# Fixed tiles for pairs and single banks, router constants inside a planned order, and new ranks in an attention, routing and gated-layer kernel

## The chip, the cores and the metric

One core of one Trainium2 chip runs the whole program. The metric is the device time of one execution in microseconds (us), lower is better; several runs are taken and their median is quoted.

## The reference

Inputs `q, k, v, a_re, a_im` have shape (4, 8, 768, 48): batch, heads, sequence, head width. A complex, decaying state per head is stepped along the sequence, then tokens are sent to experts, and a gated layer follows.

```python
mag = np.sqrt(a_re * a_re + a_im * a_im)
scale = np.minimum(mag, 0.999) / (mag + 1e-06)
a_re_n, a_im_n = (a_re * scale, a_im * scale)
for t in range(S):
    new_re = ar * S_re - ai * S_im
    new_im = ar * S_im + ai * S_re
    S_re, S_im = (new_re + k_t v_t^T, new_im)
    y[:, :, t] = q_t @ S_re
...
logits = x @ w_gate            # x: 3072 tokens x 384
# pairs (token, expert) in falling order of logit; each expert takes 384 tokens
out[mask] = np.maximum(x[mask] @ w1[e], 0.0) @ w2[e]
...
return ((x @ w_a) * (x @ w_b)) @ w_out
```

## The kernel before

**Stages.** `whole` calls `make_router` (constants and small tiles of the routing), then `attention`, then `moe_glu` (experts and gated layer, eight phases). The change touches the first two.

**How attention is tiled.** The sequence is cut into 6 chunks of 128, the batch into 2 pairs, so there are 12 steps `i` (NB), each with 2 units `n` (24 units). For each step `gates` (L304) loads a_re, a_im, q, k and v and forms logarithms and angles: `ln`, `rec`, `rho`, `g`, `e`, `th` on ScalarE and VectorE (L331, L334, L338). `sums` (L352) takes running sums along the chunk by matrix products: the sum of logarithms `LL` (L376 to L389, by the helper on L361) and of angles `HH` (L395 to L398); each holds a pair of banks of the accumulation memory (PSUM). `turned` (L401) makes rotated q and k (`nat`, L420 to L429). `factor` (L448) makes the factor between chunks, with small rows that are copied by DMA (L349, L434) and a swap of halves (`sw`, L503, L504). `unit` (L510) transposes q and k (`TT`, a pair of banks, L526, copied out on L529), makes scores (`S`, L538) that VectorE masks into `Ab` (L540), the outer product for the state (`X`, L549 to L558), the output (`Y`, L566 inside the chunk, L573 from the state before, copied out as `yT` on L579) and the projection (`O`, L586), from which come the logits (L588) and the rows `xo` that GpSimd stores (L591, L593).

**What sets the order.** `Plan` (L55) is a planner in Python. `add` registers a step with an engine letter, a duration, what it reads and writes, a due time, and the PSUM place that it takes or drops. `order` (L87) runs a list simulation: among the engines' waiting steps it takes the one that can start first, and among those that can start at that moment on one engine the lowest rank (due time times STRETCH, less the tail of work behind it with the same due time, plus an offset EARLIER for its kind). An engine is never left idle for a better step. `issue` (L173) emits the steps in that order. VectorE, ScalarE and TensorE then keep the order of emission by hand (L615); SyncE (SP, the loads and copies) and GpSimd are ordered by the compiler's own scheduler. In the trace that one follows the order of the program among what is ready.

**Places.** Four tiles `bank` of [128, 2, 512] are the eight banks; a single-bank result gets one half of such a tile, preferably beside a half in use (L117), and a pair gets a whole tile (L115), where at most two of the long pairs (LL, HH) may be open (L112, L113). In the planner loads are on engine `S` with 2.3 us each and 2.2 us until they have landed; the small copies of rows are on an engine `R` of their own with 0.1 us, although the chip issues both from SP. HOP, 0.15 us, is the price of handing over between engines. A change of ScalarE's activation table adds SWITCH (146) to a rank.

**Constants of the router.** `make_router` issues them at once, before `attention` (L737 to L800): iotas and memsets on GpSimd, small operations on VectorE (`iot1` L740, `e8` L748, `rows` L752, `offs` L754, `j96` L758, four copies `fold` L768). `attention` issues its own constants after them: `Ws` and `Wt` (L227 to L234), and in `late_setup` (L269) memsets of `vb`, `Sb`, `qkT`, `mask` and `iw` on GpSimd. `ident` (L629) comes before all.

Of the kernel before, what the change touches and what calls it, by code (L numbers as in the profile page):

```python
# [33 lines left out]
SWITCH = 146.0  # L34
HOP = 0.15
LANDING = 2.3
SPLIT_PAIRS = 2
EARLIER = {'Acc': -467, 'Ae': 116, 'Aea': 12, 'Afw': 18, 'Ag': -78, 'Aln': -89, 'Apb': 12, 'AqkT': -59, 'Arec': 193, 'As2': -144, 'Asf': 114, 'Asn': 207, 'Ath': 85, 'Axo': 118, 'AyT': 340, 'G-': -187, 'PF': -234, 'PHH': 106, 'PLL': 27, 'PO': -143, 'PS': 257, 'PTT': -30, 'PX': -50, 'PY': 4, 'Rends': 91, 'Rfw': 64, 'Rsw': -16, 'Sim': -202, 'Sqk': -12, 'Sre': -160, 'Sv': -72, 'V-': -90, 'VAb': -133, 'VS': -213, 'Ve': 49, 'Vearly': -54, 'Veb': -31, 'Vft': -38, 'Vg': 6, 'Vlg': -112, 'Vn4': -129, 'Vnat': -174, 'Vr': 187, 'Vrho': 46, 'Vrt0': 173, 'Vrt1': -94, 'Vxs': 198}
STRETCH = 2.818752
LONG = ("LL", "HH")  # L40
ENGINES = "PVASGR"
SLOW = 1.08
SINGLE = 1
LOAD = 2.3
LAND = 2.2
PATIENCE = 9.0
ENOUGH = 20.5
BUFS = {'rho': 2, 'e': 2, 'ea': 2, 'r': 2, 's2': 2}
# [6 lines left out]
class Plan:  # L55
# [3 lines left out]
    def __init__(self, banks):  # L59
        self.tasks, self.writer, self.readers = [], {}, {}  # L60
        self.banks = banks
        self.held, self.at_of, self.inuse = {}, {}, set()
# [24 lines left out]
    def order(self):  # L87
# [5 lines left out]
        for t in reversed(T):  # L93
            own = [T[u]["tail"] for u in users[t["n"]] if T[u]["due"] == t["due"]]
            t["tail"] = t["dur"] + t["land"] + HOP + max(own, default=0.0)
            t["rank"] = t["due"] * STRETCH - t["tail"] + EARLIER.get(t["kind"], 0.0)
# [8 lines left out]
        open_at = [0.0] * 8  # L105
# [12 lines left out]

        while any(waiting.values()):
# [26 lines left out]
            if t["take"]:  # L146
                can = [x for x in places(t["take"]) if x[0] <= at + 1e-9]
                t["banks"] = holds[t["take"]] = min(can, key=lambda x: (x[1], x[0]))[2]
                for b in t["banks"]:
                    open_at[b] = None  # L150
# [7 lines left out]
            if t["drop"]:  # L158
                for b in holds.pop(t["drop"]):
                    open_at[b] = end + HOP  # L160
# [3 lines left out]
            for u in users[n]:  # L164
                left[u] -= 1
                ready_at[u] = max(ready_at[u], end + t["land"] + (HOP if T[u]["eng"] != e else 0.06))
# [6 lines left out]
    def issue(self, load_table):  # L173
        self.used = [0.0] * 8
        for at, n, table in self.order():
# [4 lines left out]
            if t["take"]:  # L180
                b = t["banks"]
                self.held[t["take"]] = (self.banks[b[0] // 2] if len(b) == 2 else self.banks[b[0] // 2][:, b[0] % 2])
                self.inuse.update(b)
                self.at_of[t["take"]] = b
            t["fn"]()
            if t["drop"]:
                self.held.pop(t["drop"])
                for b in self.at_of.pop(t["drop"]):
                    self.inuse.discard(b)
                    self.used[b] = at  # L190

    def spare(self):
        b = min((b for b in range(8) if b not in self.inuse), key=lambda b: self.used[b])
        return self.banks[b // 2][:, b % 2]


def attention(tc, q, k, v, a_re, a_im, wg, x_dram, consts, L, guard, router, tail_work=None):
# [8 lines left out]
    with ExitStack() as st:  # L206
# [9 lines left out]
        plan = Plan(many(ps, 4, [128, 2, 512], "bank"))  # L216
# [87 lines left out]
        def gates(i, due):  # L304
# [4 lines left out]
            a = dict(due=due)  # L309
            for us in parts(i):  # L310
# [3 lines left out]
                for nm, t, src in (("re", ld_re, a_re), ("im", ld_im, a_im)):  # L314
                    plan.add("S", took(LOAD, us), lambda t=t, src=src, r=r, at=at, d2=d2: SP.dma_start(t[j][:, r], flat(src, at, d2)),
                             writes=[(nm, j, u) for u in us], due=due - 20 - 40 * (i < 2), land=LAND)
            for x, src in ((0, q), (1, k)):
                plan.add("S", LOAD, lambda x=x, src=src: SP.dma_start(ld_qk[j][:, x], flat(src, base, dims)),
                         writes=[("qk", j, x)], due=due - 10, land=LAND)
            plan.add("S", LOAD, lambda: SP.dma_start(vb[j].rearrange("p u h d -> p (u h) d")[:, :, 0:D], flat(v, base, dims)),  # L320
                     writes=[("v", j)], due=due - 4, land=LAND)
# [24 lines left out]
            if c:  # L346
                f = fw[i % 4]
                for slot, t, nm in ((6, e, ke), (7, th, kth)):
                    plan.add("R", 0.1, lambda t=t, slot=slot: SP.dma_start(f[:, slot], t[0:1].rearrange("p (r d) -> p r d", d=D)),  # L349
                             [nm + (0,), nm + (1,)], [("fw", i % 4, slot)], land=LANDING, **a)  # L350

        def sums(i, due):  # L352
# [17 lines left out]
            for us in parts(i):  # L370
# [5 lines left out]
                plan.add("P", 0.65 * m, lambda us=us: mm(kL, Ws, e, us, True), K(ke) + ([] if first else [kL + (0,)]), K(kL), **first, **a)  # L376
# [8 lines left out]
                plan.add("A", took(0.95, us), lambda us=us: A.activation(by(ea[:, 0], us), p(kL, us), AF.Exp, bias=bias["shift"]),  # L385
                         K(kL), K(kea + (0,)), table="E", **a)
                plan.add("P", 0.17 * m, lambda us=us: mm(kL, eye["twice"], cc, us, False, True), K(kcc), K(kL), **a)
                plan.add("A", took(0.95, us), lambda us=us: A.activation(by(ea[:, 1], us), p(kL, us), AF.Exp, bias=bias["shift"], scale=-1.0),
                         K(kL) + ([kea + (1, 0)] if done and len(us) == 1 else []), K(kea + (1,)), table="E", **done, **a)  # L389
            for us in parts(i):  # L390
# [4 lines left out]
                plan.add("P", 0.65 * len(us), lambda us=us: mm(kH, Wt, th, us, True, True), K(kth) + ([] if first else [kH + (0,)]), K(kH), **first, **a)  # L395
# [5 lines left out]
        def turned(i, due):  # L401
# [31 lines left out]
            def row(dst, key, t, reads, at):  # L433
                plan.add("R", 0.1, lambda: SP.dma_start(dst, t[at:at + 1].rearrange("p (r d) -> p r d", d=D)),  # L434
# [13 lines left out]
        def factor(i, due):  # L448
# [19 lines left out]
            plan.add("V", 0.75, one, kf[0:4], [kw, kf[0], kf[2]], **a)  # L468
# [6 lines left out]
            plan.add("V", 0.6, two, [kw] + kf[4:6], [kw], **a)  # L475
# [15 lines left out]
            plan.add("P", 0.25, turn, [kw], [kp], take=kp, **a)  # L491
            plan.add("A", 0.2, lambda: A.activation(b.rearrange("p a u h -> p (a u h)"), held[kp][0:96, 0:32], AF.Copy),
                     [kp], [("pb", i % 2)], drop=kp, **a)
            for u in range(2):
# [10 lines left out]
                plan.add("R", 0.1, swap, [("rt1", z)], [("sw", z)], land=LANDING, **a)  # L505
# [4 lines left out]
        def unit(n, due):  # L510
# [7 lines left out]
            for h4 in range(2):  # L518
# [9 lines left out]
                plan.add("P", 0.89, turn, kn, [kT], take=kT, **a)  # L528
                plan.add("A", 0.95, lambda h4=h4, kT=kT: A.activation(  # L529
                    qt[0:96, 4 * h4:4 * h4 + 4], held[kT][0:96].rearrange("p y (a s t) -> p (y a) s t", a=2, s=2), AF.Copy),  # L530
                    [kT], [("qkT", m, h4)], drop=kT, **a)
            for h4 in range(2):
# [6 lines left out]
                plan.add("P", 0.92, scores, [("qkT", m, h4)], [kS], take=kS, **a)  # L539
# [3 lines left out]
            if c < NCK - 1:  # L543
# [7 lines left out]
                plan.add("P", 1.36, outer, kn[2:4] + [("v", j)], [kX], take=kX, **a)  # L551
# [23 lines left out]
            plan.add("P", 0.5, lambda: inside(0), [("Ab", m, 0), ("v", j)], [(kY, 0)], take=kY, **a)  # L575
            plan.add("P", 0.5, lambda: inside(1), [("Ab", m, 1), ("v", j), (kY, 0)], [(kY, 1)], **a)
            if c:
                plan.add("P", 0.96, before, [("S", b), (kY, 0)] + [("qkT", m, x) for x in range(2)], [(kY, 1)], **a)
# [8 lines left out]
            plan.add("P", 0.95, out, [("yT", m)], [kO], take=kO, **a)  # L587
# [20 lines left out]
        plan.add("V", 1.7, bounds, [("ends", NB - 1, 0), ("ends", NB - 1, 1)], [], due=PERIOD * (NB + 1))  # L608
        early = router.early(lambda: held[("Q",)], slice(0, 12))

        for x in range(8):
            plan.add("V", 0.3, lambda: next(early, None), ["early"] + [("lg", n) for n in range(12)], ["early"],
# [122 lines left out]


# [832 lines left out]
```

## Time and profile before

| What | us |
|---|---|
| median of 3 runs | 1108.28 (1104.43 to 1112.72) |
| profiled execution | 1107.54 |
| its span, first to last instruction | 1105.9 |
| TensorE busy | 991.6 (90%) |
| VectorE busy | 655.9 (59%) |
| ScalarE busy | 486.5 (44%) |
| GpSimd busy | 168.7 (15%) |

Busy shares are means over stages with different limits: the attention stage ends at about 327 us, and the layers behind it are a second regime. In rows, PE is TensorE's products, PEld its loads of weights, DVE VectorE, ACT ScalarE, POOL GpSimd and SPq SyncE's queue of DMAs. An idle time in brackets stands before the instruction, with what ended it.

### The profile page before, as it was taken

What the parts mean: (1) busy time and instruction counts of PE and PEld (TensorE: products, weight loads), DVE (VectorE), ACT (ScalarE), POOL (GpSimd) and SP (SyncE); (2) the same over time, 40 slices, a digit from 0 to 9 for tenths busy, and PEclk for the clock granted to TensorE, in tenths of its full rate; (3) what the DMA queues carried; (4) which work ended last, traced back from release to release, by engine and by line L of the source; (5) the groups of instructions that cost most, each with busy time, mean ns of one, the idle gap of its engine ahead of it and who ended that gap; (6) DMA issues with size and microseconds to landing.
All of it is one profiled execution on the core that took longest, in us unless ns stands there. A gap on an engine that the chain in (4) does not pass through costs nothing.

```text
span 1105.9 us, 17272 instructions
## 1 busy us (share of the span) xinstructions
PE 991.6 (90%) x6587; PEld 902.8 (82%) x6587; DVE 655.9 (59%) x1632; ACT 486.5 (44%) x870; POOL 168.7 (15%) x217
## 2 busy tenths in 40 slices
PE   1788988998963899699999999999999999999994
PEld 0566767777753788589999998999999999999994
DVE  5567768887856889873445546635545545433321
ACT  5786867887722544353233233233233224333321
POOL 6000000000003203030320311212122032212001
PEclk9898989998995899799999999999999999999997
DMA  9954555643114435420310211211121031211000
GB/s 129 141 104 98 112 98 105 114 99 71 41 56 156 122 115 196 119 79 8 100 44 15 86 40 33 79 36 44 37 67 56 1 100 55 82 36 37 8 1 25
DMA packets 146619, 81.49 MB, mean 74 GB/s; under 512 B 130400, under 2 KB 132320, under 8 KB 146528
## 3 DMA queue, kind: packets, MB, share of 16 engines
q1 hardware_dynamic: 134304, 40.97, 18.4%
q0 software_dynamic: 12224, 39.34, 11.0%
q8 instruction: 53, 0.87, 0.3%
q14 instruction: 38, 0.31, 0.1%
HBM read 67.65 MB, written 9.44 MB: 70 GB/s over the span
## 4 chain that ended last, share of the span: by engine, by line
PE 67%; issue 20%; DVE 6%; POOL 3%; ACT 2%; DMA 2%; SPq 0%; POOLq 0%; DVEq 0%; ACTq 0%
PE mm L1213 28%; PE acc L1161 8%; PE acc L1162 7%; PE acc L1163 7%; PE mm L1161 3%; PE mm L1162 3%; PE mm L1163 3%; PE bank L361 2%; PE bank L538 1%; POOL x_rows L593 1%; DVE stage L713 1%; DVE stage L715 1%; PE bank L549 1%; PE mm L1141 1%; DMA raw<-moe_w_in,i 1%
## 5 line engine op out<-in xcount | busy, mean ns | idle before, releaser
L1246 DVE TENSOR_TENSOR g<-mm,a_s 128x384 f32<-128x384 f32 x96 | 53.3, 556 | 153.8 <-PE mm L1213 130.9
L1065 ACT ACTIVATE gh<-g 128x384 fp32r<-128x384 f32 x96 | 50.3, 525 | 159.5 <-DVE g L1246 148.9
L1241 ACT ACTIVATE a_s<-mm 128x384 f32<-128x384 f32 x96 | 47.1, 490 | 156.1 <-PE mm L1213 145.5
L1161 PE MATMUL acc<-woh,gh 128*128 128x384 f32 x288 | 97.1, 343 | 1.0 <-ACT woh L717 1.0
L1162 PE MATMUL acc<-wol,gh 128*128 128x384 f32 x288 | 97.0, 337 | 0.0
L1163 PE MATMUL acc<-woh,gl 128*128 128x384 f32 x288 | 96.6, 337 | 0.0
L1114 POOL DMA_INDIRECT raw<-moe_w_in,i x64 | 66.3, 1036 | 197.5 <-DVE w2l L1066 109.3
L1213 PE MATMUL mm<-yh,wbh 128*128 128x384 f32 x288 | 72.9, 352 | 4.0 <-ACT wbh L717 3.6
L1066 DVE TENSOR_TENSOR gl<-g,gh 128x384 fp32r<-128x384 f32 x96 | 53.5, 557 | 38.6 <-ACT gh L1065 37.6
L1213 PE MATMUL mm<-yh,wah 128*128 128x384 f32 x288 | 72.9, 354 | 3.5 <-ACT wah L717 3.4
L1161 PE MATMUL mm<-xh,w1h 128*128 128x384 f32 x192 | 67.6, 352 | 1.8 <-DVE xl L1066 1.3
L1213 PE MATMUL mm<-yl,wah 128*128 128x384 f32 x288 | 68.7, 342 | 0.0
L1213 PE MATMUL mm<-yh,wal 128*128 128x384 f32 x288 | 68.1, 343 | 0.0
L1213 PE MATMUL mm<-yh,wbl 128*128 128x384 f32 x288 | 67.6, 340 | 0.0
L1213 PE MATMUL mm<-yl,wbh 128*128 128x384 f32 x288 | 66.9, 339 | 0.0
L1162 PE MATMUL mm<-xl,w1h 128*128 128x384 f32 x192 | 65.9, 343 | 1.0 <-DVE xl L1066 1.0
L1162 PE MATMUL acc<-hl,w2h 128*128 128x384 f32 x192 | 65.1, 339 | 1.7 <-DVE hl L1188 1.7
L1163 PE MATMUL mm<-xh,w1l 128*128 128x384 f32 x192 | 65.6, 342 | 0.0
L1161 PE MATMUL acc<-hh,w2h 128*128 128x384 f32 x192 | 65.0, 349 | 0.0
L1163 PE MATMUL acc<-hh,w2l 128*128 128x384 f32 x192 | 64.6, 336 | 0.0
L1100 POOL DMA_INDIRECT raw<-moe_w_in,i x24 | 24.7, 1029 | 234.7 <-DVE left L978 168.8
L1065 ACT ACTIVATE w1h<-raw 128x384 fp32r<-128x384 f32 x64 | 32.7, 522 | 59.9 <-PE mm L1162 54.3
(288 smaller groups left out, 2389.4 us busy)
## 6 DMA issues: line engine op xcount, KB each, us to landing
vb<-v_in SPq DMA_DIRECT2D x12, 384.0 KB, 5.1
ld_qk<-q_in SPq DMA_DIRECT2D x12, 384.0 KB, 4.1
ld_qk<-k_in SPq DMA_DIRECT2D x12, 384.0 KB, 4.7
x_rows<-xo POOLq DMA_DIRECT2D x24, 192.0 KB
stage<-moe_w_a_in SPq DMA_DIRECT2D x12, 384.0 KB, 3.2
stage<-moe_w_b_in SPq DMA_DIRECT2D x12, 384.0 KB, 3.2
stage<-moe_w_out_in SPq DMA_DIRECT2D x12, 384.0 KB, 3.0
ld_im<-a_im_in SPq DMA_DIRECT2D x11, 384.0 KB, 5.7
```

The costliest lines, as they stand in the source:

```text
L361: PE.matmul(held[key][:, u, 0:HD], w, t[:, u * HD:u * HD + HD], start=first, stop=last, skip_group_check=True)
L538: PE.matmul(p[:, x], qt[0:96, 4 * h4 + x, 1], qt[0:96, 4 * h4 + x, 0], start=True, stop=True)
L1065: a = A.activation(hi, src, AF.Copy)
L1066: return a, V.tensor_tensor(lo_, src, hi, op=OP.subtract)
L1100: G.indirect_dma_start(out=raw[:, j], out_offset=None, in_=w1r, in_offset=bass.IndirectOffsetOnAxis(ap=i1[:, j:j + 1], axis=0))
L1114: G.indirect_dma_start(out=raw, out_offset=None, in_=w2r, in_offset=bass.IndirectOffsetOnAxis(ap=i2[:, f:f + 1], axis=0))
L1161: PE.matmul(p, lh, rh, start=first, stop=False)
L1162: PE.matmul(p, lh, rl, start=False, stop=False)
L1163: PE.matmul(p, ll, rh, start=False, stop=last)
L1213: PE.matmul(p, a[:, j, c], b[:, j], start=(n == 0), stop=(n == 8))
L1241: A.activation(a_s, pa, AF.Copy)
L1246: V.tensor_tensor(g, pb, a_s, op=OP.mult)
```

## The change

- Two pairs of banks are tiles of their own (`pair`, [128, 2, 512]) and the other four banks are single tiles (`bank`, [128, 512]). LL, HH and TT share the two pairs; all else shares the four single ones. SPLIT_PAIRS goes to 3, which no longer limits anything.
- The router's constants become a list `todo` of 28 functions, which `attention` registers as steps of VectorE (0.2 us each, one chain, due at the third period); `early` also waits for the last. GpSimd's part of a constant is issued inside its step.
- The planner puts the copies of rows on `S` with 0.55 us (1.15 for the swap), the loads after the first two steps at 0.6 us and 3.8 until landing. HOP is by engine (0.22 after TensorE, 0.08 after others), LANDING 1.5 instead of 2.3, SLOW 1.03 instead of 1.08, some durations change by hundredths.
- STRETCH, SWITCH, ENOUGH and all offsets EARLIER have new values. Second buffers: `ln` and `g` get one, `r` and `s2` lose theirs.

```diff
-SWITCH = 146.0
-HOP = 0.15
-LANDING = 2.3
-SPLIT_PAIRS = 2
-EARLIER = {'Acc': -467, 'Ae': 116, ...}
-STRETCH = 2.818752
+SWITCH = 13.0
+HOP = {"P": 0.22, "V": 0.08, "A": 0.08, "S": 0.08, "G": 0.08}
+NPAIR = 2
+LANDING = 1.5
+SPLIT_PAIRS = 3
+EARLIER = {'Acc': 8, ..., 'Sim': 10, ..., 'Sre': -1, ..., 'Vsetup': -4, 'Vxs': 4}
+STRETCH = 0.844334
-ENOUGH = 20.5
-BUFS = {'rho': 2, 'e': 2, 'ea': 2, 'r': 2, 's2': 2}
+ENOUGH = 8.5
+BUFS = {'rho': 2, 'ln': 2, 'g': 2, 'e': 2, 'ea': 2}
...
-                return [(max(open_at[b], open_at[b + 1]), 0, (b, b + 1)) for b in range(0, 8, 2)
-                        if open_at[b] is not None and open_at[b + 1] is not None]
-            return [(open_at[b], 0 if open_at[b ^ 1] is None else 1, (b,)) for b in range(8) if open_at[b] is not None]
+                return [(open_at[b], b) for b in range(NPAIR) if open_at[b] is not None]
+            return [(open_at[b], b) for b in range(NPAIR, 8 - NPAIR) if open_at[b] is not None]
...
-        plan = Plan(many(ps, 4, [128, 2, 512], "bank"))
+        plan = Plan(many(ps, NPAIR, [128, 2, 512], "pair") + many(ps, 8 - 2 * NPAIR, [128, 512], "bank"))
...
+            load, land = (2.3, 2.2) if i < 2 else (0.6, 3.8)
...
-                    plan.add("R", 0.1, lambda t=t, slot=slot: SP.dma_start(f[:, slot], t[0:1].rearrange("p (r d) -> p r d", d=D)),
+                    plan.add("S", 0.55, lambda t=t, slot=slot: SP.dma_start(f[:, slot], t[0:1].rearrange("p (r d) -> p r d", d=D)),
...
-                plan.add("R", 0.1, swap, [("rt1", z)], [("sw", z)], land=LANDING, **a)
+                plan.add("S", 1.15, swap, [("rt1", z)], [("sw", z)], land=2.4, **a)
...
+        for f in router.setup:
+            plan.add("V", 0.2, f, ["setup"], ["setup"], due=PERIOD * 3)
         early = router.early(lambda: held[("Q",)], slice(0, 12))
...
+    todo = []
+    def do(f):
+        todo.append(f)
     iot = cs.tile([128, 128], F32, name="iot")
-    G.iota(iot, pattern=[[1, 128]], base=0, channel_multiplier=0, allow_small_or_imprecise_dtypes=True)
+    do(lambda: G.iota(iot, pattern=[[1, 128]], base=0, channel_multiplier=0, allow_small_or_imprecise_dtypes=True))
     iot1 = cs.tile([128, NTHR], F32, name="iot1")
-    V.tensor_scalar(iot1, iot[:, 0:NTHR], 1.0, None, op0=OP.add)
+    do(lambda: V.tensor_scalar(iot1, iot[:, 0:NTHR], 1.0, None, op0=OP.add))
...
     for g in range(4):
-        G.memset(same4[32 * g:32 * g + 32, g], 1.0)
-        V.tensor_copy(fold[32 * g:32 * g + 32], ident[32 * g:32 * g + 32, 32 * g:32 * g + 32])
+        do(lambda g=g: G.memset(same4[32 * g:32 * g + 32, g], 1.0))
+        do(lambda g=g: V.tensor_copy(fold[32 * g:32 * g + 32], ident[32 * g:32 * g + 32, 32 * g:32 * g + 32]))
...
+    R.setup = todo
```

## Rows read from the trace of the kernel before

**Rows 1.** The page's slices of the span: clock granted to TensorE, in tenths

```profile
PEclk9898989998995899799999999999999999999997
```

**Rows 2.** Busy time of PE, PEld, DVE, ACT, POOL, then clock, DMA share, GB/s

```profile
40.00:310.00 270.00, 241.45 (x2056) 197.25 (x2056) 206.01 (x388) 205.86 (x297) 11.55 (x22) 0.95 0.49 96
```

**Rows 3.** Timeline of the start: start us, us, engine, line, operation, [idle before]

```profile
8.02 0.47 DVE L740 TENSOR_SCALAR iot<-iot 128x32 f32<-128x32 f32 x1
...
8.48 0.51 ACT L331 ACTIVATE g<-rho 128x384 f32<-128x384 f32 x1
...
9.02 0.61 ACT L331 ACTIVATE g<-g,b_one 128x384 f32<-128x384 f32 x1
...
9.46 4.73 DVE L768 COPY fold<-ident 32x32 f32<-32x32 f32 x4
...
15.70 0.57 DVE L334 SCALAR_TENSOR_TENSOR g<-ln,g 128x384 f32<-128x384 f32 x1
...
18.25 1.62 PE L361 MATMUL bank<-e,Ws 128*128 128x384 f32 x2 [18.25 <-POOL iw L283]
```

**Rows 4.** The same timeline, GpSimd's instructions

```profile
1.18 0.24 POOL L738 IOTA iot<- 128x128 f32 x1
...
4.59 0.19 POOL L780 TENSOR_SCALAR_AFFINE_SELECT third<-third 48x3 bf16<-48x3 bf16 x1
...
9.99 3.58 POOL L275 MEMSET qkT<- 32x2048 f32 x2
...
14.09 0.48 POOL L279 MEMSET iw<- 128x416 f32 x1
```

**Rows 5.** TensorE's waits, 18 to 327 us: total us, times, longest

```profile
PE bank L566 <- DVE Ab L540: 8.8, 14, 1.2
...
PE bank L489 <- ACT qkT L529: 4.5, 2, 2.7
...
PE bank L566 <- ACT qkT L529: 0.3, 1, 0.3
```

**Rows 6.** Timeline of the steady part, TensorE and VectorE

```profile
207.91 1.16 PE L538 MATMUL bank<-qkT 96*128 96x128 f32 x8
209.00 1.09 PE L573 MATMUL bank<-qkT,Sb 128*64 128x128 f32 x16
...
210.14 0.69 DVE L540 TENSOR_TENSOR Ab<-bank,mask 128x512 f32<-128x512 f32 x1 [1.11 <-PE bank L573]
...
210.89 0.66 PE L566 MATMUL bank<-Ab,vb 128*64 128x128 f32 x8 [0.25 <-DVE Ab L540]
```

**Rows 7.** Timeline of the stage's end, ScalarE and TensorE

```profile
320.10 0.60 ACT L579 ACTIVATE yT<-bank 128x512 f32<-128x512 f32 x1 [7.09 <-PE bank L566]
...
320.75 1.09 PE L573 MATMUL bank<-qkT,Sb 128*64 128x128 f32 x16 [0.74 <-ACT yT L579]
```

**Rows 8.** Groups by line and shape, 0 to 330 us: busy us, mean ns

```profile
L529 ACT ACTIVATE qkT<-bank 96x1024 f32<-96x1024 f32 x48 | 47.3, 1016 | 3.1 <-PE bank L526 3.0
...
L616 ACT ACT_TABLE_LOAD x23 | 29.5, 1283 | 0.3
```

**Rows 9.** Timeline of one step: the holds of the pairs, and r

```profile
205.84 1.56 PE L361 MATMUL bank<-e,Ws 128*128 128x384 f32 x4
...
211.48 1.56 PE L361 MATMUL bank<-th,Wt 128*128 128x384 f32 x4
...
206.70 0.83 ACT L417 ACTIVATE sn<-r 128x768 f32<-128x768 f32 x1
...
220.68 0.90 ACT L388 ACTIVATE ea<-bank,b_shift 128x768 f32<-128x768 f32 x1
...
218.26 0.94 DVE L396 TENSOR_SCALAR r<-bank 128x768 f32<-128x768 f32 x1
219.24 0.96 DVE L398 TENSOR_TENSOR r<-bank,r 128x768 f32<-128x768 f32 x1
```

**Rows 10.** VectorE's waits, 18 to 327 us

```profile
DVE Sb L507 <- DMA sw<-rtb: 16.5, 11, 4.2
```

More of the change, by code (lines that the diff above doesn't have):

```diff
@@ L147, in order @@
                 can = [x for x in places(t["take"]) if x[0] <= at + 1e-9]
-                t["banks"] = holds[t["take"]] = min(can, key=lambda x: (x[1], x[0]))[2]
-                for b in t["banks"]:
-                    open_at[b] = None
+                t["place"] = holds[t["take"]] = min(can)[1]
+                open_at[t["place"]] = None
             load = 0.0
@@ L158, in order @@
             if t["drop"]:
-                for b in holds.pop(t["drop"]):
-                    open_at[b] = end + HOP
+                open_at[holds.pop(t["drop"])] = end + HOP[t["eng"]]
             free[e] = end
@@ L180, in issue @@
             if t["take"]:
[L181 to L184, printed above, removed]
+                self.held[t["take"]] = self.banks[t["place"]]
+                self.at_of[t["take"]] = t["place"]
             t["fn"]()
@@ L467, in one @@
                 V.tensor_tensor(w[:, 5], w[:, 1], w[:, 2], op=OP.subtract)
-            plan.add("V", 0.75, one, kf[0:4], [kw, kf[0], kf[2]], **a)
+            plan.add("V", 0.92, one, kf[0:4], [kw, kf[0], kf[2]], **a)
             def two():
@@ L474, in two @@
                 V.tensor_tensor(w[:, 7], w[:, 1], w[:, 2], op=OP.add)
-            plan.add("V", 0.6, two, [kw] + kf[4:6], [kw], **a)
+            plan.add("V", 0.66, two, [kw] + kf[4:6], [kw], **a)
             def three():
@@ L538, in scores @@
                         PE.matmul(p[:, x], qt[0:96, 4 * h4 + x, 1], qt[0:96, 4 * h4 + x, 0], start=True, stop=True)
-                plan.add("P", 0.92, scores, [("qkT", m, h4)], [kS], take=kS, **a)
+                plan.add("P", 0.9, scores, [("qkT", m, h4)], [kS], take=kS, **a)
                 plan.add("V", 0.69, lambda h4=h4, kS=kS: V.tensor_mul(
@@ L550, in outer @@
                                   start=True, stop=True)
-                plan.add("P", 1.36, outer, kn[2:4] + [("v", j)], [kX], take=kX, **a)
+                plan.add("P", 1.41, outer, kn[2:4] + [("v", j)], [kX], take=kX, **a)
                 def keep(kX=kX):
@@ L586, in out @@
                     PE.matmul(p[:, jj, 0:104], yT[m][:, jj], iw[:, jj], start=True, stop=True)
-            plan.add("P", 0.95, out, [("yT", m)], [kO], take=kO, **a)
+            plan.add("P", 0.89, out, [("yT", m)], [kO], take=kO, **a)
             plan.add("V", 0.17, lambda: V.tensor_reduce(
@@ L771, in make_router @@
     under = cs.tile([48, 4, 8], F32, name="under")
-    G.memset(under, 0.0)
     third = cs.tile([48, 3], BF, name="third")
-    G.memset(third, 1.0)
-    for a in range(3):
-        for i in range(2):
-            G.affine_select(under[:, i:i + 3:2], under[:, i:i + 3:2], pattern=[[-1, 2], [-2, 8]], compare_op=OP.not_equal,
-                            fill=1.0, base=-16 * a, channel_multiplier=1)
-    G.affine_select(third, third, pattern=[[-16, 3]], compare_op=OP.is_ge, fill=0.0, base=0, channel_multiplier=1)
@@ L780, in make_router, with unders @@
-    G.affine_select(third, third, pattern=[[16, 3]], compare_op=OP.is_ge, fill=0.0, base=15, channel_multiplier=-1)
+    def unders():
+        G.memset(under, 0.0)
+        G.memset(third, 1.0)
+        for a in range(3):
+            for i in range(2):
+                G.affine_select(under[:, i:i + 3:2], under[:, i:i + 3:2], pattern=[[-1, 2], [-2, 8]],
+                                compare_op=OP.not_equal, fill=1.0, base=-16 * a, channel_multiplier=1)
+        G.affine_select(third, third, pattern=[[-16, 3]], compare_op=OP.is_ge, fill=0.0, base=0, channel_multiplier=1)
+        G.affine_select(third, third, pattern=[[16, 3]], compare_op=OP.is_ge, fill=0.0, base=15, channel_multiplier=-1)
@@ L787, in make_router @@
         As = rk.tile([LT, NT, E], BF, name="As")
[L788 removed]
+        do(lambda: V.memset(As, 0.0))
     else:
```

104 lines of the change are left out of this document (51 added, 53 removed).

## The prediction, made before the change was run

> **What bounds the kernel now.** I read the page first. Its clock row [rows 1] shows TensorE granted nearly full speed except in the thirteenth slice, which lies behind the attention stage. Then I asked for busy time by stretch [rows 2]. The changed code orders only the attention stage, from 0 to about 327 us; the 779 us after it hold routing, expert layers and the gated layer, which the change does not touch. So any gain or loss must be made in the first 327 us. In its steady part, 40 to 310, TensorE is busy 241.45 of 270 us (89%), VectorE 206.01 and ScalarE 205.86 (76% each). TensorE is the nearest bound, and what can be won there is its 28.55 us of idle time plus what the clock of 0.95 costs. Next, the timeline of the first microseconds [rows 3]: TensorE does no real work before 18.25 us. Last, the waits by engine [rows 5] and two close looks at who holds whom [rows 6, 7].
>
> The sum is made against the profiled execution: 1107.54 us, of which 1105.9 is the span. The median of the three runs, 1108.28, lies 0.74 above it. A measurement of this kernel can tell about 1% from no change, some 11 us: faster means below 1097.2, slower above 1119.4.
>
> **The start.** ScalarE has the logarithm of the first unit ready at 9.02 + 0.61 = 9.63 us; VectorE takes it up (L334) only at 15.70. In those 6.07 us VectorE works off the router's constants, from L740 at 8.02 to the four `fold` copies of L768, which alone take 4.73 us [rows 3]. The change makes them steps of the plan. Two readings of what then happens are far apart. If the constants leave VectorE's front, the chain to TensorE starts 6.1 us earlier: one end of the range. But follow the planner: the 28 steps form one chain whose first is ready at time zero, and VectorE has nothing else ready until the first loads have been planned in. The planner gives an idle engine whatever can start first, whatever its rank. Three loads of half a pair (1.15 + 0.08 each) and a landing of 2.2 bring the first `rho` to about 5.97 in the plan; steps of 0.2 + 0.06 fill that with 23 of 28, all the dear ones among them. So they still stand ahead of `rho` on VectorE, now in an order fixed by hand. And `iot` and `jr`, which feed them, now come on GpSimd after the memsets of `late_setup` in program order; in the trace they run at 1.18, ahead of those [rows 4]. If GpSimd keeps program order among what is ready, `iot` runs behind the `iw` memset, which ends at 14.57; less the router's constants that no longer precede it, which lie between 1.18 and 4.59 + 0.19 = 4.78 (some 3.3 us, an estimate, since a few of the kernel's own lie among them) [rows 4]: about 11.3. VectorE then needs 1.4 us for L740 to L758 (8.02 to 9.46) and 0 to 4.73 for `fold` [rows 3]: `rho` starts at 12.7 to 17.4. The first g on VectorE follows after `rho` itself (about 0.6, as L334's half tile of 0.57) and 1.15 of ScalarE (8.48 to 9.63), at 14.5 to 19.2 against 15.70: between 1.2 won and 3.5 lost. I take 0 for the start, inside the second reading, and keep -6.1 and +4 for the range. The moved steps issue no DMA; on GpSimd they are passed only by `late_setup`, and the one engine queued behind them is VectorE.
>
> A rule of the Trainium skill bears on the `fold` copies. They last 4.73 us in all beside the two `qkT` memsets of 3.58 us on GpSimd [rows 3, 4]. SBUF — State Buffer, section "Who interferes with whom", says that some VectorE copies and GpSimd share one port pair, and that the later one is blocked for the whole instruction of the other. By that rule the copies would again cost up to 4.7 us if they still run beside memsets, and the start would be lost time as now; the trace agrees with it as far as one overlap can.
>
> **The banks.** Before, four tiles of two banks are handed out by halves. Two places show that a half is held up by the other half. At 207.91 TensorE makes scores (L538, 1.16 us, done by 209.07); VectorE's masking of them (L540) starts only at 210.14, when the 1.09 us of L573 for another unit end, and is put down to it; TensorE's next L566 waits for that masking [rows 6]. And at 320.75 L573 starts 0.74 us late, as ScalarE's yT (320.10 + 0.60) ends, although L573 reads nothing of it [rows 7]. Tiles of one bank each take that coupling from all single-bank results. Its price in the trace: from 18 to 327 us TensorE waits for the last reader of some bank, and not for its own inputs, in 12 rows of the waits that add up to 15.1 us (the dearest is L489 behind L529 with 4.5, the cheapest L566 behind L529 with 0.3); besides, L566 waits 8.8 us in 14 pieces for L540, its true input, which the same coupling makes late [rows 5]. Together 23.9 us at most. Some of these are plain reuse of a full bank and come back with six places instead of eight. Between 0 and 23.9 I take half, 12 us, because the close look [rows 6] shows one masking late by 1.07 us and only 0.25 us of it reaching TensorE, while [rows 7] shows a wait that reaches it whole.
>
> **The pairs.** The sums of logarithms (LL), the angles (HH) and the transposes (TT) now share two pairs where they had four. In one step of the steady part LL is open from 205.84 to 220.68 + 0.90 = 221.58 (15.7 us) and HH from 211.48 to 219.24 + 0.96 = 220.20 (8.7 us) [rows 9]. Four transposes per step hold a pair for their copy of 1.02 us (L529) [rows 8] and about as long for TensorE's part, 8.2 us in all. That is 32.6 us of pair time in a step of some 24 (12 steps in the 287 us from 40 to 327), against 48 on offer. It fits, and in that step no transpose runs while both are open. So 0 in the sum, but the cover is thin: without it every second transpose waits for the copy before it, L529 with 1016 ns [rows 8], and over 24 units that is 24.4 us, the other end.
>
> **Order, SP and buffers.** The new ranks move every step; what that is worth by itself no row shows. What the planner knows better (SP's own issue time, handover by engine, a shorter landing) matters only where a load ends a wait: VectorE waits 16.5 us for the state's exchange `sw` in 11 pieces [rows 10], on an engine with 64 us to spare; 0, with 0 to -5 kept inside the 23.9. Rows and loads now stand in one SP order; a row copy that waits for its source can hold a load, but loads are a step ahead. A lower price for changing the activation table could add loads of 1.28 us to the present 23 [rows 8]; ScalarE has 64 us free in 270, so even eight more (10 us) cost nothing unless one falls into a chain. Taking the second buffer from `r` and `s2`: the last reader of `r` starts at 206.70 and the next writer at 218.26 [rows 9], over 10 us of slack; 0. The second `ln` and `g` only loosen.
>
> **The sum.** 1107.54 + 0 (start) - 12 (banks) + 0 (pairs) + 0 (the rest) = 1095.5 us, 1.15% under the median. Its own range, with a third to two thirds of the 23.9 and the start between -1 and +2, is about 1090 to 1101.
>
> **The rivals.**
> *The start is won too.* If GpSimd takes `iot` first, as it does now [rows 4], VectorE does the constants while the loads land, and 6.1 us come on top: 1089.4. For it speaks that the first iota needs nothing; against it that it now comes later in the program than ten memsets that need nothing either.
> *The waits change their name.* TensorE is at 89%, two engines at 76%, and the data chains (masking, copies) stay as long as they are. If the coupled waits were hidden behind those, the engine meets the next input instead: 15.1 us become waits for inputs, and the time is 1107 with nothing done. That the constants stay ahead of `rho` is the part of the change that would not do what it says.
> *The pairs starve.* Slower: LL holds one pair through most of each step, transposes pass one by one through the other, and TensorE meets L529's 1.02 us twelve to twenty-four times: 1107.5 + 24.4 - 12 = 1120 with the bank gain, more without. It decides from the point where the wait exceeds 12 us in all, 0.5 us per unit. The 15.7 us hold of LL speaks for it, the step of [rows 9], which already lives with two pairs, against it. The Trainium skill, Perfetto Trace Analysis, section "Optimization Strategy", says that gaps repeating on the engine that should be saturated can mean that PSUM has no place for the next tile; that speaks for this rival, and no run yet shows it.
>
> **How the numbers follow.** My forecast gets 0.42, of which two thirds lie below 1097.2 (0.27) and the rest within 1% (0.15). The start won too: 0.16, all faster. Waits renamed: 0.20, within 1%. Pairs starving: 0.22, all slower. So faster 0.43, the same 0.35, slower 0.22. The range goes from 1078 (1107.5 less 6.1 and all 23.9) to 1120, the middle of the slower case, and leaves about 0.1 above and little below.
>
> **What would show it.** Right: first TensorE work still near 18 us, VectorE's L334 soon after the moved constants; masking right after its scores; waits of L573 and L566 behind yT, xo and xs gone; end of attention some 12 us before 327. Wrong start: first TensorE work near 12. Wrong pairs: waits of L526 and of L361 behind L529 or L398 that add up to over 12 us. Wrong altogether: TensorE's idle time in the steady part above 28 us.

## The result and the profile after

The changed kernel takes 1073.05 us (median of 4 runs, 1071.15 to 1073.87); the kernel before, in runs on the same chip, 1110.5 us. The ratio is 0.9669, 95% interval 0.964 to 0.9699: faster, by nearly three times the gain that was forecast, and below the range.

In the code after the change most lines moved up by seven: sums and angles are L354 (L361 before), transposes L519 (L526) and their copy L522 (L529), scores L531 (L538), masking L533 (L540), L559 and L566 the two products of a unit (L566, L573), yT L572 (L579), the output product L579 (L586).

The page of the changed kernel, its span and the clock granted to TensorE, to be held against [rows 1]:

```profile
span 1072.3 us, 17244 instructions
...
PEclk9999999999956998799999999999999999999997
```

Eleven slices at 9 now stand where [rows 1] has twelve, a mixture of 8 and 9; the dip of the routing stage comes one slice earlier, because the attention stage ends earlier. TensorE's work next to that end, in the timeline of each kernel: first the last output product of the attention stage and the first product of the routing (L890) after the change, then the routing's first product (L884) before it.

```profile
290.51 1.14 PE L579 MATMUL bank<-iw,yT 128*128 128x104 f32 x8 [0.69 <-ACT yT L572]
...
293.18 0.98 PE L890 MATMUL bank<-oh,cmp 128*32 128x8 bf16 x24 [1.53 <-DVE cmp L885]
```

```profile
327.15 0.98 PE L884 MATMUL bank<-oh,cmp 128*32 128x8 bf16 x24 [2.35 <-DVE cmp L879]
```

327.15 - 293.18 = 34.0 us; the profiled executions differ by 1107.54 - 1073.87 = 33.7. So all of it was won in the attention stage. Busy time by stretch (columns as in [rows 2]): the attention stage after the change with its steady part, then the same stage before it. The first and the last of these rows hold the same 2199 groups of products.

```profile
20.00:292.00 272.00, 254.91 (x2199) 205.82 (x2199) 222.09 (x418) 227.44 (x331) 12.50 (x23) 0.99 0.58 105
40.00:280.00 240.00, 230.66 (x2058) 190.71 (x2058) 206.27 (x390) 209.18 (x301) 11.96 (x22) 0.99 0.57 107
```

```profile
18.00:327.00 309.00, 265.60 (x2199) 212.54 (x2199) 223.45 (x420) 226.74 (x330) 14.29 (x28) 0.95 0.51 96
```

TensorE is idle 272 - 254.91 = 17.1 us instead of 309 - 265.60 = 43.4: 26.3 us. The other 10.7 us is the same work done faster: 254.91/265.60 = 0.960, and the granted clocks stand as 0.95/0.99 = 0.960. The start gave a little back (2.4 us, below).

TensorE's waits in the stage after the change, 18 to 295 us (columns as in [rows 5]; the first row is the start):

```profile
PE pair L354 <- DVE e L327: 20.7, 1, 20.7
PE pair L354 <- ACT th L324: 4.1, 2, 3.3
PE bank L559 <- DVE Ab L533: 2.7, 4, 1.4
...
PE pair L519 <- ACT qkT L522: 1.4, 2, 1.1
...
PE pair L354 <- DVE r L389: 0.7, 1, 0.7
```

Of the 15.1 us in which a last reader of some bank held TensorE [rows 5] only small pieces are left, the dearest these 1.4 and 0.7 us; waits behind xo and xs are gone; the wait for the masking fell from 8.8 to 2.7. Why the masking is earlier shows in what VectorE waited for ahead of it. The view of line L533 of the changed kernel, then of L540 of the kernel before:

```profile
  PE bank L531: 9.8, 9
  ACT ea L381: 3.2, 5
```

```profile
  PE bank L538: 14.1, 8
  ACT yT L579: 3.6, 1
  PE bank L566: 2.3, 4
  PE bank L549: 1.9, 3
  PE bank L573: 1.1, 1
  PE bank L586: 0.7, 2
  PE bank L361: 0.5, 1
```

Before, 10.1 us in 12 pieces went to yT and to five kinds of products that make no scores; after, none does. (L566 reads `Ab`, so its 2.3 us may in part be a true wait for the buffer; the other 7.8 are no business of the masking.) The 3.2 us put down to `ea`, which the masking doesn't read, are most likely waits for its own scores too: in the timeline at 141 us the scores end at 140.09 + 1.05 = 141.14, `ea` at 140.29 + 0.90 = 141.19, and the masking starts at 141.26; the other four places lie alike.

### The profile page after: what moved, and what is told of

Read it like the earlier page. It is cut to its first block, busy times and chain, and to the rows that moved or that the text cites. A ratio compares the mean times of both kernels' runs of the same rounds, so it can differ in the third digit from the quotient of the medians.

```text
span 1072.3 us, 17244 instructions
## 1 busy us (share of the span) xinstructions
PE 981.7 (92%) x6587; PEld 896.9 (84%) x6587; DVE 649.8 (61%) x1632; ACT 486.9 (45%) x870; POOL 168.1 (16%) x217
## 3 DMA queue, kind: packets, MB, share of 16 engines
q0 software_dynamic: 12224, 39.34, 11.3%
```

## The experiments

Each time is a median; ratios are to the kernel before in the same series of runs. The runs were spread over several chips, and the kernel before has a median of 1109.75 to 1113.31 us in the five series, so a difference of times from two series can be off by some 4 us; where it matters, the difference by the ratios stands beside it. "Idle" is TensorE's idle time in 40 to 280 us, worked out as 240 less its busy time there.

| run | us | ratio, 95% interval | idle | clock there |
|---|---|---|---|---|
| kernel before | 1110.5 | 1 | 26.8 | 0.94 |
| changed kernel | 1073.05 | 0.9669 [0.964, 0.9699] | 9.3 | 0.99 |
| halves | 1080.47 | 0.9732 [0.9688, 0.9776] | 14.7 | 0.99 |
| before_apart | 1088.41 | 0.981 [0.9765, 0.9856] | 16.5 | 0.95 |
| consts_at_once | 1068.48 | 0.9622 [0.958, 0.9664] | 9.6 | 0.98 |
| iota_first | 1063.81 | 0.9593 [0.9549, 0.9636] | 8.9 | 0.99 |
| old_numbers | 1139.32 | 1.0267 [1.0218, 1.0317] | 40.0 | 0.88 |
| new_numbers | 1108.01 | 0.9982 [0.9954, 1.0009] | 23.7 | 0.97 |
| old_ranks | 1130.08 | 1.0176 [1.0114, 1.0239] | 40.8 | 0.94 |
| old_costs | 1113.51 | 1.0033 [1.0003, 1.0062] | 25.5 | 0.93 |
| nudge_a | 1116.03 | 1.0059 [1.0035, 1.0084] | 29.2 | 0.94 |
| nudge_b | 1098.53 | 0.9891 [0.9849, 0.9933] | 20.8 | 0.95 |
| no_ranks | 1134.97 | 1.024 [1.0192, 1.0288] | 36.0 | 0.90 |
| sp_uncounted | 1093.39 | 0.9855 [0.9803, 0.9908] | 20.0 | 0.95 |
| nudge_a_halves | 1131.17 | 1.0157 [1.012, 1.0193] | 36.5 | 0.94 |
| no_ranks_halves | 1153.81 | 1.0357 [1.0323, 1.0392] | 40.2 | 0.88 |
| before_nudged | 1148.52 | 1.0319 [1.0284, 1.0354] | 45.3 | 0.93 |

### What the freed halves are worth, in the new and in the old order

**halves**: the changed kernel, each engine's order kept; the four singles are halves of two tiles again.

```diff
-        plan = Plan(many(ps, NPAIR, [128, 2, 512], "pair") + many(ps, 8 - 2 * NPAIR, [128, 512], "bank"))
+        four = many(ps, 4, [128, 2, 512], "bank")
+        plan = Plan(four[:2] + [t[:, x] for t in four[2:] for x in range(2)])
```

> The changed kernel with its order of instructions unchanged on every engine, but the four single banks are again halves of two tiles of two banks. Theory A (the coupling of the halves of a tile cost most of the 37 us): most of it comes back, 1095 to 1105 us, and waits of L559, L566 and L533 behind readers and writers of the other half return. Theory B (the new ranks and the planner's better numbers are worth the most, the tiles a few us): 1075 to 1082 us.

**before_apart**: the kernel before; after each step is issued, the dependences between its instructions and those on the other half of its tile are taken out where no data passes. The order of TensorE, VectorE, ScalarE and GpSimd is kept. SP's order of DMAs shifts with it at four places, where ten of its 225 issues change places with near neighbours; this run can't separate what that is worth.

```diff
+            for bs in mine:
+                if len(bs) == 1:
+                    for ins in self.log:
+                        for old, of in self.seen[bs[0] ^ 1]:
+                            if ins.engine == old.engine or of in t["after"]:
+                                continue
+                            self.tc.declare_no_dep(ins, old, reason="the other bank of the tile")
```

> The kernel before, with the order of TensorE, VectorE, ScalarE and GpSimd kept, but the dependence between instructions on different halves of one tile of banks is taken away where no data passes between them. Theory A: 1080 to 1092 us. Theory B: 1100 to 1108 us, since the old order keeps its waits for inputs.

Measured: in the new order the coupling costs 1080.47 - 1073.05 = 7.4 us, in the old one 1111.89 - 1088.41 = 23.5 (16 to 26 by the interval): theory B held in the new order, theory A in the old one. The view of VectorE's masking line in `halves` (lines are one further down there) shows the coupled waits back, smaller than before the change:

```profile
  PE bank L580: 2.8, 3
  ACT ea L382: 1.3, 2
  PE bank L560: 1.2, 1
```

Neither L580 nor L560 makes scores (L560 reads `Ab`, so its part may be a true wait). How the gain of `before_apart` is made up shows in its stage, held against the stage before it above:

```profile
18.00:307.00 289.00, 259.41 (x2199) 209.29 (x2199) 221.76 (x419) 226.21 (x330) 13.91 (x27) 0.96 0.55 103
...
307.79 0.96 PE L924 MATMUL bank<-oh,cmp 128*32 128x8 bf16 x24 [1.53 <-DVE cmp L919]
```

From 18 us to the routing's first product TensorE is idle 307.79 - 18 - 259.41 = 30.4 us instead of 327.15 - 18 - 265.60 = 43.6, and the same products take 6.2 us less. The two make 19.4 us; the profiled executions differ by 1107.54 - 1088.21 = 19.3.

What follows: the mechanism is real in both; its price is not a property of the tiles alone. In the old order the coupling explains 23.5 of some 38 us; the rest, from 1088.4 down, must come from what else the change does. Taken the other way round, the new order with its halves coupled gives 1111.89 - 1080.47 = 31.4 us, and freeing them only the last 7.4.

### The start

**consts_at_once**: the changed kernel, the router's constants issued at once as before the change, empty steps in their place in the plan. **iota_first**: only the two iotas that feed VectorE, `iot` and `jr`, are issued at once, and the plan has two steps fewer. In both, TensorE and ScalarE keep the order of the changed kernel; SP's shifts by single places.

```diff
-        todo.append(f)
+        todo.append(f if given is not None else f() and None or (lambda: None))
```

```diff
-    do(lambda: G.iota(iot, ...
+    G.iota(iot, ...
...
-    do(lambda: G.iota(jr, ...
+    G.iota(jr, ...
```

> The changed kernel with the router's constants issued ahead of attention as before, the planned order of all else kept (empty steps stand in their place). If the moved constants cost time, as the start of the changed trace shows (first running sum on TensorE at 20.66 against 18.25 us): 1069 to 1072 us. If they were a gain: 1076 to 1082 us.

> The changed kernel with only the two iotas that feed VectorE's constants (iot, jr) issued at once, ahead of the memsets of late_setup on GpSimd; all else as it is. If VectorE's wait for iot (11.7 us) sets the start and the stage behind it is shifted as a whole: first running sum near 11 us, 1063 to 1066 us. If the first loads or another chain take over behind it, or the steady part swallows it: 1069 to 1073 us.

Measured: 1068.48 and 1063.81, 4.6 and 9.2 us below the changed kernel; the first is half a microsecond better than its range, the second inside it. The timeline of the start, first of the changed kernel, then of `iota_first`:

```profile
6.43 3.55 POOL L267 MEMSET qkT<- 32x2048 f32 x2
...
14.42 0.24 POOL L739 IOTA iot<- 128x128 f32 x1
...
14.70 0.18 DVE L741 TENSOR_SCALAR iot<-iot 128x32 f32<-128x32 f32 x1 [11.69 <-POOL iot L739]
...
15.84 0.72 DVE L768 COPY fold<-ident 32x32 f32<-32x32 f32 x4
...
16.92 0.56 DVE L331 TENSOR_TENSOR rho<-ld_im,rec 128x384 f32<-128x384 f32 x1
...
20.66 1.62 PE L354 MATMUL pair<-e,Ws 128*128 128x384 f32 x2 [20.66 <-DVE e L327]
```

```profile
1.19 0.24 POOL L739 IOTA iot<- 128x128 f32 x1
2.35 0.27 DVE L741 TENSOR_SCALAR iot<-iot 128x32 f32<-128x32 f32 x1
...
3.92 0.80 DVE L768 COPY fold<-ident 32x32 f32<-32x32 f32 x4
6.30 0.56 DVE L331 TENSOR_TENSOR rho<-ld_im,rec 128x384 f32<-128x384 f32 x1
...
10.04 1.62 PE L354 MATMUL pair<-e,Ws 128*128 128x384 f32 x2 [10.04 <-DVE e L327]
```

In the changed kernel VectorE stands for 11.69 us, its order fixed, at a constant whose iota GpSimd reaches only behind all of `late_setup`; `rho` is queued behind it and starts at 16.92, though ScalarE's part of its input is there at 5.3 us, and in `iota_first` it starts at 6.30. With the two iotas ahead the constants fill the time of the first loads, and TensorE starts 20.66 - 10.04 = 10.6 us earlier, of which 9.2 reach the end. `iota_first` is the best version found: it beats the kernel before by 4% and the changed one by 0.9% (its slowest run, 1066.80, lies below the fastest of the changed kernel, 1071.15).

### What the new order rests on

The remaining gain could lie in the six fixed places, in the planner's prices, in the ranks, or in their fit to each other. Four kernels mix old and new; `R` stands for the queue that the planner before did not count.

**old_numbers**: tiles, places and planned constants of the changed kernel, the planner's numbers as before. **new_numbers**: the reverse, tiles, places and constants of the kernel before, the numbers new. (SPLIT_PAIRS and the durations that the change corrects by hundredths stay with the tiles in both.) **old_ranks** and **old_costs**: the changed kernel with only one group of numbers taken back.

```diff
old_ranks:
-SWITCH = 13.0
+SWITCH = 146.0
-STRETCH = 0.844334
+STRETCH = 2.818752
-ENOUGH = 8.5
+ENOUGH = 20.5
...
old_costs:
-HOP = {"P": 0.22, "V": 0.08, "A": 0.08, "S": 0.08, "G": 0.08}
+HOP = {e: 0.15 for e in "PVASGR"}
-LANDING = 1.5
+LANDING = 2.3
-SLOW = 1.03
+SLOW = 1.08
...
-                plan.add("S", 1.15, swap, [("rt1", z)], [("sw", z)], land=2.4, **a)
+                plan.add("R", 0.1, swap, [("rt1", z)], [("sw", z)], land=LANDING, **a)
```

> The changed kernel with its tiles, places and planned constants, but with all of the planner's numbers as before (prices, handover, landing, ranks, stretch, SP not counted, buffers of e, r, s2). Theory A, the rest of the gain comes with the numbers: what is left is the old order with the coupling gone (1088.4 measured with the halves declared independent) plus 4.6 for the moved constants, about 1093; at least 1086, and TensorE idle in 40 to 280 at least 18 us. Theory B, the rest comes with the six fixed places whatever the numbers: within 8 us of the changed kernel, 1073 to 1081, idle at most 14 us. Rival: the old numbers were fitted to eight interchangeable halves and starve the two pairs; then over 1100, and TensorE's transposes and first products of LL and HH wait for pair readers over 12 us.

> The kernel before with its four two-bank tiles, its places chosen freely and its constants at once, but with all of the new numbers of the planner. Theory A (numbers): the changed kernel plus 7 for coupled halves less 4.6 for the constants, about 1076; at most 1086. Theory B (places): the order needs the fixed places, so 1095 or more, near the kernel before less little. In both, waits of TensorE for readers of another half come back.

> The changed kernel with only SWITCH, STRETCH, ENOUGH and EARLIER as before (names of SP's steps adapted). Theory A1, the ranks carry the gain: 1086 or more. Theory A2, the prices and the counting of SP carry it: at most 1078. If the two only work together: between, with over 1078 in this run and in the one with old prices.

> The changed kernel with only the planner's HOP, LANDING, SLOW, load prices and the uncounted SP queue as before, ranks new (names of SP's steps adapted). Theory A1 (ranks carry the gain): at most 1078. Theory A2 (prices and SP carry it): 1086 or more. VectorE's waits for the state's exchange sw, 5 us in the changed kernel and 16.5 before, would be nearer 16 if the counting of SP is what shortened them.

Measured: 1139.3, 1108.0, 1130.1 and 1113.5. None of the four keeps the gain, so neither "the numbers carry it" nor "the places carry it" holds; the old ranks alone or the old prices alone are enough to lose all of it. `old_numbers` met its rival: TensorE's waits there, 18 to 362 us,

```profile
PE pair L519 <- ACT qkT L522: 9.2, 9, 2.6
PE pair L354 <- ACT ea L378: 7.7, 4, 3.3
PE pair L354 <- DVE r L391: 6.1, 3, 3.7
...
PE pair L519 <- ACT ea L381: 1.2, 2, 0.8
```

The first, third and last are waits for a pair's reader, 16.5 us; the second may be a reader or the next link of the same unit's chain, and with it the sum is 24.2. That is the starving of the pairs that the prediction feared, and it comes with ranks that were made for eight free halves. In the changed kernel the same rows came to some 3 us.

If the gain is a fit of ranks to planner and tiles, small steps off it must lose it.

**nudge_a**, **nudge_b**: each entry of EARLIER (there are 44; the expectations say 45) moved by 2, up or down at random. **no_ranks**: EARLIER empty. **sp_uncounted**: only SP's queue uncounted again.

```diff
nudge_a:
-EARLIER = {'Acc': 8, 'Aea': 5, ...
+EARLIER = {'Acc': 6, 'Aea': 3, ...
no_ranks:
-EARLIER = {'Acc': 8, 'Aea': 5, ...
+EARLIER = {}
sp_uncounted:
-ENGINES = "PVASG"
+ENGINES = "PVASGR"
-                plan.add("S", 1.15, swap, [("rt1", z)], [("sw", z)], land=2.4, **a)
+                plan.add("R", 0.1, swap, [("rt1", z)], [("sw", z)], land=2.4, **a)
```

> The changed kernel with each of the 45 corrections of EARLIER moved by 2, up or down at random. The last runs gave 1108 to 1139 for every mixture of old and new numbers. Theory F, the new ranks are one well-fitted order among many that the same planner can give: a nudge of 2 loses most of the gain of the order, 1085 to 1115, TensorE idle in 40 to 280 at least 18 us. Theory G, the planner's corrected prices and tiles hold good for any sensible ranks: within 7 us of 1073.

> As nudge_a with another random draw. Theory F: 1085 to 1115, and other than nudge_a by several us. Theory G: within 7 us of 1073.

> The changed kernel with EARLIER empty: the rank is due time and tail alone, with the new prices. Theory F (the fit carries the gain): 1100 to 1140, like the mixtures. Theory G (prices and tiles carry it): 1073 to 1085.

> The changed kernel with only SP taken out of the planner's engines again (its steps cost 0.1 and are never queued, as before); landing, handover, slowness and ranks new. Theory F: any such edit gives another order out of the fit, 1085 to 1115, with VectorE's wait for sw not the place of the loss. Theory H, the counting of SP is worth its own time: over 1085 too, but VectorE's wait for sw goes from 5 us to 11 or more and the loss is found behind it. If SP's count is neither: within 7 us of 1073.

Measured: 43.0, 25.5, 61.9 and 20.3 us above the changed kernel. (`nudge_a` is a microsecond past the top that theory F gave it.) So the gain of the order is its fit: two microseconds of rank, in steps whose due times lie 22 apart, cost more than the whole change brought in one draw and two thirds of it in the other.

`sp_uncounted` tells more, because a good part of its loss can be followed. VectorE's wait for the exchange `sw` is at 16.5 us in 11 pieces, as before the change [rows 10], against 4.6 in the changed kernel, and TensorE's wait for the masking at 10.8 against 2.7. Its timeline, where one leads to the other:

```profile
142.93 0.54 DVE L492 TENSOR_TENSOR rtb<-xs,pb 96x384 f32<-96x384 f32 x1
...
144.12 2.05 SPq L342 DMA_DIRECT2D fw<-e  x1
...
146.26 0.54 SPq L496 DMA_DIRECT2D sw<-rtb  x1
146.85 0.58 SPq L497 DMA_DIRECT2D sw<-rtb  x1
...
150.08 0.56 DVE L500 TENSOR_TENSOR Sb<-rta,sw 96x384 f32<-96x384 f32 x1 [3.14 <-DMA sw<-rtb]
150.56 1.75 DVE L413 TENSOR_TENSOR eb<-ea,ld_qk 128x1536 f32<-128x1536 f32 x1
...
152.69 0.68 DVE L533 TENSOR_TENSOR Ab<-bank,mask 128x512 f32<-128x512 f32 x1
...
153.43 1.12 PE L559 MATMUL bank<-Ab,vb 128*64 128x128 f32 x8 [2.57 <-DVE Ab L533]
```

The same chain stands at 180.27 (2.84) and 206.97 (2.52): three places make 7.9 of TensorE's 10.8 us. `rtb` is ready at 143.47; SP, held by a row copy until 146.17, issues the exchange from 146.26 to 147.43, where this planner has 0.1 us and no queue. So it believed the exchange there sooner than it came, and put the masking behind the step that waits for it.

The kernel before has the same thing, with another step behind it. After its longest wait for `sw`, VectorE gets late to `n` (L377), the rounded sum for which TensorE stands:

```profile
153.76 0.55 DVE L507 TENSOR_TENSOR Sb<-rta,sw 96x384 f32<-96x384 f32 x1 [4.16 <-DMA sw<-rtb]
...
155.31 0.95 DVE L377 TENSOR_SCALAR n<-bank 128x768 bf16<-128x768 f32 x1
...
156.31 0.80 PE L361 MATMUL bank<-n,eye_minus 128*128 128x384 bf16 x2 [3.42 <-DVE n L377]
```

With the waits right behind four more exchanges, at 101.48 (1.85), 180.24 (1.17), 204.16 (1.92) and 250.56 (0.62), that is 9.0 us of TensorE's idle time in the kernel before; in the changed kernel two such waits are left, at 124.83 (1.39) and 167.20 (0.37). This is what the order of VectorE's queue shows; what else would have held TensorE there isn't shown.

The exchange is not all of the loss, and its wait does not set the time alone. TensorE's waits behind the copy of a transpose (L354 and L519 behind `qkT`) are 7.7 us in `sp_uncounted` against 1.8 in the changed kernel, and these views show no link from them to `sw`. In `new_numbers` VectorE waits only 1.7 us for `sw`, and the kernel takes 1108.0. In `old_costs` it waits 13.4, nearer to 16 as expected, but TensorE waits only 2.5 for the masking.

### Does the price of coupling go with the order?

**nudge_a_halves** and **no_ranks_halves**: `nudge_a` and `no_ranks` with the edit of `halves`. **before_nudged**: the kernel before, each entry of EARLIER moved by 40, up or down at random.

```diff
-EARLIER = {'Acc': -467, 'Ae': 116, ...
+EARLIER = {'Acc': -507, 'Ae': 76, ...
```

> nudge_a with its four single banks again halves of two two-bank tiles: every engine's order stays that of nudge_a (1116.0). Coupled halves cost 22 to 23 us in the old order and 7.4 in the new one. Theory B1, the low price belongs to the fitted order alone: here 12 to 25 us more, 1128 to 1141. Theory B2, six fixed places with the two pairs apart are what makes coupling cheap, whatever the order: 4 to 10 us more, 1120 to 1126.

> no_ranks (1135.0) with its four single banks again halves of two tiles, nearly the same order (two neighbours on VectorE and on SP change places). Theory B1: 1147 to 1160. Theory B2: 1139 to 1145.

> The kernel before with each correction of EARLIER moved by 40, up or down at random (its corrections are some twenty times those of the change, in range too). If the old ranks were as well fitted to the old planner as the new ones to the new: 20 us more or worse, 1130 to 1155, so the gain of the change is that of one fit over another on better tiles. If the old ranks were no fit at all: 1095 to 1120, and the gain is that a fit is there now.

Measured: coupling costs 1131.17 - 1116.03 = 15.1 us and 1153.81 - 1134.97 = 18.8 us in these two orders (in the second, two neighbours on VectorE and two on SP change places as well). These are times of two series on two chips. By the ratios the four prices are 7.0 us in the fitted order, 10.9 in that of `nudge_a`, 13.0 in that of `no_ranks` and 21.1 in the old one. By the times theory B1 holds for both; by the ratios the first lies between the theories. So the price is clearly higher in the old order than in the fitted one; that it is higher in the two others as well is likely, but not clear of the noise. The old ranks were a fit too: nudged, they lose 1148.52 - 1113.31 = 35.2 us in the one draw tried.

## Why the prediction was wrong

**The sign and the place were right, the size was not**: 12 us forecast, 33.7 in the profiled execution. By the steps of the sum:

- *The start, 0 taken.* The second reading held in each of its links: constants ahead of `rho`, `iot` behind `late_setup`, first g on VectorE at 18.71, inside the 14.5 to 19.2 given. It cost 2.4 us at TensorE (18.25 to 20.66). `iot` came at 14.42, not at the estimated 11.3, because the copies and DMAs of `iw` also ran ahead of it; the `fold` copies took 0.72 us, near the low end of their 0 to 4.73. The two nearly cancel, so that the start came inside its range is in part luck. The rival "won too" is what `iota_first` does.
- *The rule on the shared port pair* (the Trainium skill, SBUF — State Buffer, section "Who interferes with whom"): the trace agrees. The four copies take 4.73 us beside the long `qkT` memsets [rows 3, 4], 0.72 in the changed kernel and 0.80 in `iota_first`, where these run at another time, and 4.59 in `consts_at_once`, where they meet again.
- *The banks, -12 taken of 23.9.* The mechanism was right: no row of after shows a masking held by a product that makes no scores. The size depends on the order: 7.4 us in the new one, 23.5 by the medians (19.3 in the profiled executions) in the old one, from whose waits the bound was read. There TensorE's idle time fell by 13.2 us, near the half that was taken; the 6.2 us by which the same products became shorter are what the term lacked, at a granted clock of 0.96 instead of 0.95. Even with all of the 23.9 the sum would have come to 1107.54 - 23.9 = 1083.6.
- *The pairs, 0 taken.* Right for this order. The estimate of 32.6 us of pair time against 48 did not make it so: `old_numbers`, with the same tiles, lost TensorE 16.5 to 24 us behind pair readers, the price that the rival named. The Trainium skill's rule on repeating gaps (Perfetto Trace Analysis, section "Optimization Strategy") fits `old_numbers`, where TensorE waits nine times, up to 2.6 us, behind the copy of a transpose, not the changed kernel, where it does so twice.
- *Order, SP and buffers, 0 taken.* This is the step that failed. Of the new ranks the prediction says "what that is worth by itself no row shows", and it put them into the sum as nothing, with no bound, though the change renews all of them. Measured: from the old order with its halves freed to the new order with its constants at once, 1088.4 - 1068.5 = 19.9 us; with the halves still coupled, and the constants where the change puts them, the new order gives 31.4. The SP term was put at nothing with "an engine with 64 us to spare", which is a mean over the stage, while VectorE works through its steps in the planned order: in `sp_uncounted` three waits of some 3 us for `sw` stood ahead of a masking each time and cost TensorE 7.9 us. That its 20.3 us are the price of the counting alone is not shown, since the order changes with it. The trace of the kernel before could have priced the term: 9.0 us of TensorE's idle time follow right behind a wait for `sw`, against the 0 to -5 allowed, and 3.8 of them (L538 behind Ab and xs) stand in the 15.1 that the prediction put down to the banks. In the changed kernel 1.8 are left.
- *The clock* had no term. 10.7 us of the 34 are TensorE's own products at 0.99 instead of 0.95. The prediction's first paragraph named the loss at 0.95 as winnable, and the sum did not come back to it.

The balance of the medians, with the kernel before as in the series of `before_apart`: 1111.9; -23.5 for free halves in the old order; -19.9 for the new order; +4.6 for the constants moved behind `late_setup`; 1073.1. This is one way through the change: with the order first, the halves are the last 7.4. The step of the order holds places and numbers together: none of the mixtures keeps the gain, and the runs don't show how it would split. *The waits change their name*, the rival without gain, did not happen: 26.3 us of TensorE's idle time are gone.

What stays open: how much of `before_apart`'s gain is its shifted order of DMAs; whether ranks searched anew for the old tiles would reach the same time, which is the rival to "a fit on better tiles"; and whether one more search with `iota_first` in place would find a better order still. None was tried.

## What to carry to other kernels

A change that renews the order of a stage by hand or by a planner needs a term of its own, bounded by the idle time of the bounding engine and by what its clock costs, even if no row prices it. Two results of one tile that different engines read should be two tiles: it is worth 7 to 24 us here in the four orders tried. When a group of steps is moved into a fixed order, look for the producer that was left outside it: here two iotas on GpSimd, worth 9 us.

## What the runs showed of the hardware

TensorE's idle time and its granted clock go together over all these runs: in 40 to 280 us the four with 8.9 to 14.7 us idle were granted 0.98 or 0.99, those with 16.5 to 29.2 us (the kernel before among them) 0.93 to 0.97, those with 36 us and more 0.88 to 0.94. It is not a rule for a single stretch; two rows of the kernel before, then the same two of the changed one (TensorE's busy time, clock, DMA share, GB/s):

```profile
80.00:100.00 20.00, 16.60 (x136) 1.00 0.63 134
100.00:120.00 20.00, 16.66 (x123) 0.83 0.45 89
```

```profile
80.00:100.00 20.00, 20.00 (x172) 1.00 0.70 134
100.00:120.00 20.00, 19.98 (x184) 1.00 0.74 139
```

With nearly the same idle time the first stretch was granted 2.4 GHz throughout and the next one a mixture with 1.2 GHz; the changed kernel, with no gaps to speak of there, was granted 2.4 GHz in both. So fewer idle microseconds of TensorE brought more than themselves: 26.3 of them came with 10.7 us from the clock in the changed kernel, and 13.2 with 6.2 in `before_apart`, where the order of the work is kept. That the gaps are what lowers the clock is read from their going together.
